# Wider score products, a bank for each PSUM tile, fewer direct down chunks and one final copy, in a cached-attention decode kernel

## The chip, the cores and the metric

The kernel runs on one core of one Trainium2 chip. The metric is the device time of one execution in microseconds. Before the change three runs took 1343.89, 1348.59 and 1349.69 us, with a median of 1348.59 us. The execution whose profile is read here took 1346.37 us, of which 1344.6 us lie between its first and its last instruction (the span).

## The reference

Two sequences, one new token each, go through attention over a cached key and value store, then a gated feed-forward net, and then through both once more with the same weights and caches. Everything is float32.

```python
B, Sq, D = 2, 1, 448;  H, Sk, Dh = 16, 4096, 256;  F = 1792
def A(x, k_cache, v_cache, wq, wo):            # k_cache, v_cache: [B, H, Sk, Dh]
    q = (x @ wq).reshape(B, Sq, H, Dh).transpose(0, 2, 1, 3)
    p = softmax(einsum("bhqd,bhkd->bhqk", q, k_cache) * Dh ** -0.5)
    o = einsum("bhqk,bhkd->bhqd", p, v_cache)
    return o.transpose(0, 2, 1, 3).reshape(B, Sq, H * Dh) @ wo
def F_(x, W_gate, W_up, W_down):
    gate, up = x @ W_gate, x @ W_up
    return (relu(gate) * up) @ W_down
x = x + A(layernorm(x), ...);  x = x + F_(layernorm(x), ...)
x = x + A(layernorm(x), ...);  x = x + F_(layernorm(x), ...)
```

The two caches hold 268 MB together, and each pass over the layers reads nearly all of them.

## The kernel before

**Work units.** One unit of attention is a head of one sequence: 4 MB of keys and 4 MB of values, each in four chunks of 1 MB. A pass has 32 units; the second pass goes through them in the opposite order, so that 22 chunks that the first pass read last can stay in SBUF (`KEPT`). All loads go to one large tile, the `arena`: 27 places of 1 MB, six blocks of four and three single ones.

**Loads.** A list fixes the order of all loads of the program, and SyncE's queue issues them in that order (`pump`, line 127). A load can be issued when its place in the arena has been released, which is when the last product that reads the old contents has run. Most loads of keys and values take a whole block of 4 MB; at the start and the end of a pass they take single chunks. Behind the units of a pass stand the weights of the feed-forward net: seven pieces `w_in`, four pieces `w_out`. At the end of the program nothing has to be released any more for them. In the middle, between the passes, 22 chunks are kept, and the weights go through the few places that are left.

**A unit in the loop** (line 416). `score` (line 303) multiplies the unit's query with a chunk of keys. A chunk holds 1024 keys, cut into two halves j of the head's 256 dimensions and four groups g of 256 keys. Products of one group write one PSUM row, 0, 32, 64 or 96, so that four groups stand in four column groups of the array; the two halves j are summed there. VectorE copies the result to SBUF (`found_s`, line 314), and `score_turn` (line 316) turns it, by a product with a few columns of the identity, so that keys lie on partitions. Then come the maximum and the exponentials, and `weigh` (line 350) multiplies the weights of four times two keys' columns with four pairs of value rows, 512 columns at a time, into `po`. `out_copy` and `out_add` (lines 368, 371) scale the two rows and add them into `row`; in the next unit `out_turn`, `out_keep` and `project` turn that row and multiply it with the output weights into `acc`. TensorE runs its instructions in the order in which they are written: the steps of the unit before (`out_turn`, `out_keep`, `project`) stand behind all four chunks' scores of a unit.

**The feed-forward net** (line 435). `proj` multiplies the normed x with the gate weights into `raw[:, 0]` (lines 447 to 460), then with the up weights into `raw[:, 1]` (line 469); gate and up are multiplied into `row`, transposed into `raw[:, 0]` again and copied back (lines 472 to 485). The down product has 14 chunks of rows. In the first pass all 14 go to `pd` in `raw[:, 1]` (line 517), four column groups side by side, each with 32 columns of weights. In the second pass seven go there; after them ScalarE copies `pd` (line 524), a product (line 250, called from line 525) adds it into the output rows `y`, and the other seven go straight into `y` with two columns each (line 522), all in the same column group. Those seven need an operand that is already scaled (`near`, `near_tails`, lines 496 to 505). At the end VectorE copies half of `y`, ScalarE the other half, and the result is stored (lines 539 to 542).

**Tiles and waits.** `po_all` and `raw` are one tile of two banks each. An instruction that writes one half of such a tile waits until readers of its other half are done.

## Time and profile before

| what | value |
|---|---|
| median of three runs | 1348.59 us (1343.89 to 1349.69) |
| profiled execution, its time and its span | 1346.37 us, 1344.6 us |
| TensorE, VectorE, ScalarE busy | 80%, 15%, 7% of the span |
| data moved by DMA | 562.71 MB, mean 419 GB/s |
| mean granted TensorE clock | 0.74 of full speed |
| score products (line 308) | 4096 instructions, 481 ns each as modelled |
| value products (line 358) | 2048 instructions, 812 ns each as modelled |

A product in float32 stands in the profile as two matmul instructions, each with its weight load. Instructions in four column groups overlap, so that the modelled time of one is several times the distance from one to the next. In a table of windows the columns are: the window, its length, the busy time of each engine with the count of its instructions, the granted TensorE clock, the mean busy share of the 16 DMA engines, and the rate in GB/s. In a timeline a row has its start, its length, the engine, the line and the operands, the count where equal ones are merged, and in brackets the idle time before it with what ended it.

### The profile page before, as it was taken

What the parts mean: (1) busy time and instruction counts of PE and PEld (TensorE: products, weight loads), DVE (VectorE), ACT (ScalarE), POOL (GpSimd) and SP (SyncE); (2) the same over time, 40 slices, a digit from 0 to 9 for tenths busy, and PEclk for the clock granted to TensorE, in tenths of its full rate; (3) what the DMA queues carried; (4) which work ended last, traced back from release to release, by engine and by line L of the source; (5) the groups of instructions that cost most, each with busy time, mean ns of one, the idle gap of its engine ahead of it and who ended that gap; (6) DMA issues with size and microseconds to landing.
All of it is one profiled execution on the core that took longest, in us unless ns stands there. A gap on an engine that the chain in (4) does not pass through costs nothing.

```text
span 1344.6 us, 18672 instructions
## 1 busy us (share of the span) xinstructions
PE 1077.4 (80%) x8328; PEld 476.1 (35%) x8328; DVE 203.3 (15%) x676; ACT 93.4 (7%) x284; POOL 47.7 (4%) x134
## 2 busy tenths in 40 slices
PE   4887889787787787887878988678786788767977
PEld 2434234332332333343334433234242333333432
DVE  1111111111111111111112211111111111111111
ACT  1000000000000000000010000000000000000001
POOL 0000000000000000000000000000000000000000
PEclk9867776667767776766778896876776777677678
DMA  9999999999999999999969999999999999999996
GB/s 398 432 431 431 428 428 432 431 427 428 430 433 432 429 429 427 431 432 421 403 255 400 436 428 431 431 427 431 429 429 434 428 429 429 429 434 429 426 418 252
DMA packets 29607, 562.71 MB, mean 419 GB/s; under 512 B 3284, under 2 KB 3416, under 8 KB 10200
## 3 DMA queue, kind: packets, MB, share of 16 engines
q1 hardware_dynamic: 29524, 561.53, 98.0%
q8 instruction: 65, 1.06, 0.3%
q14 instruction: 14, 0.11, 0.0%
q10 hardware_dynamic: 4, 0.00, 0.0%
HBM read 561.52 MB, written 0.00 MB: 418 GB/s over the span
## 4 chain that ended last, share of the span: by engine, by line
PE 65%; DMA 15%; another core or an unknown queue 14%; DVE 3%; issue 2%; ACT 1%; SPq 0%; POOL 0%; POOLq 0%; DVEq 0%; ACTq 0%
PE raw L308 22%; PE po L358 20%; PE small L321 11%; DMA arena<-in_k_cache_dram 11%; PE pq L283 4%; DMA arena<-in_w_head_dram 4%; PE small L380 2%; PE acc L399 2%; DVE found_s L314 2%; PE pq L286 1%; PE raw L447 1%; DMA arena<-in_w_in_dram 1%; PE raw L517 0%; PE acc L522 0%
## 5 line engine op out<-in xcount | busy, mean ns | idle before, releaser
L308 PE MATMUL raw<-arena,q 128*1 128x256 f32 x4096 | 360.2, 481 | 176.3 <-DMA arena<-in_k_cache_dram 140.0
L358 PE MATMUL po<-arena,probs 128*2 128x512 f32 x2048 | 343.9, 812 | 48.0 <-DMA arena<-in_v_cache_dram 43.1
L308 PEld LDWEIGHTS raw<-arena,q 128*1 128x1 f32 x4096 | 91.9, 91 | 376.3 <-issue 147.1
L321 PEld LDWEIGHTS small<-ident,found_s 128*128 128x128 f32 x1024 | 176.2, 248 | 123.1 <-issue 118.8
L321 PE MATMUL small<-ident,found_s 128*128 128x4 f32 x1024 | 196.2, 301 | 0.3
L314 DVE COPY found_s<-raw 128x256 f32<-128x256 f32 x256 | 108.6, 424 | 475.1 <-PE raw L308 474.6
L358 PEld LDWEIGHTS po<-arena,probs 128*2 128x2 f32 x2048 | 63.7, 103 | 293.3 <-issue 271.8
L372 DVE SCALAR_TENSOR_TENSOR row<-po,ri,row 128x256 f32<-128x256 f32 x64 | 31.0, 484 | 379.8 <-ACT row L369 379.8
L283 PE MATMUL pq<-xs,arena 128*128 128x2 f32 x384 | 71.6, 303 | 0.4 <-DVE xs L246 0.4
L283 PEld LDWEIGHTS pq<-xs,arena 128*128 128x128 f32 x384 | 68.9, 263 | 1.9 <-DVE total L256 1.5
L335 ACT ACTIVATE nm<-top,nsr 128x1 f32<-128x1 f32 x64 | 18.8, 294 | 726.2 <-POOL top L330 726.2
L330 POOL PARTITION_ALL_REDUCE top<-mx x64 | 22.5, 351 | 1184.7 <-DVE mx L328 1152.3
L369 ACT ACTIVATE row<-po,ri 128x256 f32<-128x256 f32 x64 | 30.3, 473 | 446.1 <-PE po L358 446.1
L399 PE MATMUL acc<-arena,oT 128*2 128x448 f32 x128 | 45.5, 804 | 8.1 <-DVE oT L389 8.1
L380 PE MATMUL small<-ones,row 128*128 128x1 f32 x256 | 48.5, 294 | 2.2 <-DVE row L372 2.2
L380 PEld LDWEIGHTS small<-ones,row 128*128 128x128 f32 x256 | 45.8, 252 | 4.9 <-DVE row L372 4.9
L286 PE MATMUL pq<-xs,arena 128*128 128x2 f32 x128 | 30.4, 307 | 0.0
L286 PEld LDWEIGHTS pq<-xs,arena 128*128 128x128 f32 x128 | 28.0, 270 | 0.0
L342 POOL PARTITION_ALL_REDUCE total<-rs x64 | 24.5, 383 | 63.5 <-ACT probs L338 63.5
L338 ACT ACTIVATE probs<-small,nm,sr 128x32 f32<-128x32 f32 x64 | 24.1, 377 | 2.1
L328 DVE TENSOR_REDUCE mx<-small 128x1 f32<-128x32 f32 x64 | 12.3, 191 | 62.9 <-PE small L321 62.9
L447 PE MATMUL raw<-arena,xs 128*32 128x448 f32 x128 | 16.6, 661 | 5.4 <-DMA arena<-in_w_in_dram 3.1
(90 smaller groups left out, 134.9 us busy)
## 6 DMA issues: line engine op xcount, KB each, us to landing
arena<-in_k_cache_dram SPq DMA_DIRECT2D x57, 4096.0 KB, 54.0
arena<-in_v_cache_dram SPq DMA_DIRECT2D x56, 4096.0 KB, 54.0
arena<-in_w_head_dram SPq DMA_DIRECT2D x31, 896.0 KB, 48.8
arena<-in_v_cache_dram SPq DMA_DIRECT2D x22, 1024.0 KB, 19.8
arena<-in_k_cache_dram SPq DMA_DIRECT2D x16, 1024.0 KB, 19.8
arena<-in_w_in_dram SPq DMA_DIRECT2D x14, 896.0 KB, 18.9
arena<-in_w_out_dram SPq DMA_DIRECT2D x4, 896.0 KB, 12.0
arena<-in_w_out_dram SPq DMA_DIRECT2D x3, 672.0 KB, 7.8
```

The lines of the kernel that those rows point to most:

```text
L283: nc.tensor.matmul(pq[:, j, :], w[:, at : at + P], xT[:, c, :], start=(c == 0), stop=False)
L286: nc.tensor.matmul(pq[:, j, :], w[:, FULL * DH : FULL * DH + P], xT[:, FULL + j, :], start=False, stop=True,)
L308: nc.tensor.matmul(raw[32 * g : 32 * g + 1, half, at : at + QN], q_of[u][:, j, :], kt[:, j, g, :], start=(j == 0), stop=(j == 1),)
L314: nc.vector.tensor_copy(found_s[:, half, :], raw[:, half, at : at + QN])
L321: nc.tensor.matmul(s_of[u][:, n : n + G], found_s[:, c % 2, e * P : (e + 1) * P], pick, start=True, stop=True,)
L342: nc.gpsimd.partition_all_reduce(r_of[u], rs, P, RED.add)
L358: nc.tensor.matmul(po_of[u][32 * t : 32 * t + 2, :], p_of[u][:, n : n + 2], vt[:, 2 * t * DH : (2 * t + 2) * DH], start=(c == 0), stop=(c ...
L369: nc.scalar.activation(row[:, :DH], po_of[u][:, :DH], AF.Copy, scale=r_of[u][:, 0:1])
L372: nc.vector.scalar_tensor_tensor(row[:, :DH], po_of.pop(u)[:, DH:], r_of[u][:, 1:2], row[:, :DH], op0=ALU.mult, op1=ALU.add,)
L380: nc.tensor.matmul(pT_of[u][:, c : c + 1], row[:, c * P : (c + 1) * P], ones, start=True, stop=True,)
L399: nc.tensor.matmul(acc[at : at + B], oT_of[h][:, c, :], wo[:, c * D : (c + 1) * D], start=(n < 3), stop=(n >= n_u - 3),)
L447: nc.tensor.matmul(p[32 * j : 32 * j + 32, :], xs[:, c, :], w[:, j * D : (j + 1) * D], start=(n == 0), stop=(n == 3),)
```

## The change

A chunk of keys now holds one half j of the 256 dimensions for four groups of 512 keys, instead of both halves for four groups of 256. So `score` issues four products of 512 columns for a chunk instead of eight of 256, and a sum is complete after two chunks. The host lays the keys out accordingly; the loads keep their sizes and their order. VectorE copies 512 columns twice in a unit instead of 256 columns four times: the first half to `found_s`, the second to `row`. `out_turn`, `out_keep` and `project` of the unit before move up in the order of a unit. `po_all` and `raw` become two tiles each, one for each bank. In the last feed-forward net 11 of the 14 down chunks go to `pd` and three straight to `y`, and the final copy is one ScalarE instruction.

```diff
-G, E = 4, 2
-QN = E * P
+G, E = 4, 4
...
-    po_all = ps_o.tile([P, 2, 2 * DH], F32, name="po")
-    nc.vector.memset(po_all, 0.0)
-
-    raw = ps_r.tile([P, 2, 2 * DH], F32, name="raw")
-    nc.vector.memset(raw, 0.0)
+    po_all = [ps_o.tile([P, 2 * DH], F32, name=f"po{k}") for k in "ab"]
+    raw = [ps_r.tile([P, 2 * DH], F32, name=f"raw{k}") for k in "ab"]
+    for bank in (*po_all, *raw):
+        nc.vector.memset(bank, 0.0)
...
         def score(u, c):
-            kt = get("k", order[u], c).rearrange("p (j g n) -> p j g n", j=2, g=G)
-            half, at = c % 2, c // 2 * QN
-            for j in range(2):
-                for g in range(G):
-                    nc.tensor.matmul(
-                        raw[32 * g : 32 * g + 1, half, at : at + QN],
-                        q_of[u][:, j, :], kt[:, j, g, :], start=(j == 0), stop=(j == 1),
-                    )
+            kt = get("k", order[u], c).rearrange("p (g n) -> p g n", g=G)
+            half, j = c // 2, c % 2
+            for g in range(G):
+                nc.tensor.matmul(
+                    raw[half][32 * g : 32 * g + 1, :], q_of[u][:, j, :], kt[:, g, :],
+                    start=(j == 0), stop=(j == 1),
+                )
             if ("k", order[u], c) not in after:
                 release("k", order[u], c)
-            nc.vector.tensor_copy(found_s[:, half, :], raw[:, half, at : at + QN])
+
+        def score_copy(u, half):
+            nc.vector.tensor_copy(row if half else found_s, raw[half])
...
         for u in range(n_u + 1):
             if_pair(score, u, 0)
-            for c in range(1, NC):
-                if_pair(score, u, c)
-                if_pair(score_turn, u, c - 1)
-            if_pair(score_turn, u, NC - 1)
+            if_pair(score, u, 1)
+            if_pair(score_copy, u, 0)
+            if_pair(out_turn, u - 1)
+            if_pair(out_keep, u - 1)
+            if_pair(score, u, 2)
+            if_pair(score, u, 3)
+            if_pair(score_copy, u, 1)
+            if_pair(score_turn, u, 0)
+            if_pair(project, u - 1)
+            if_pair(score_turn, u, 1)
             if_pair(softmax_max, u)
             if_pair(softmax_exp, u)
-            if_pair(out_turn, u - 1)
-            if_pair(out_keep, u - 1)
-            if_pair(project, u - 1)
...
-            near = row[:, D : D + 12 * B].rearrange("p (m j b) -> p m j b", m=FULL, j=4)
+            near = row[:, D : D + 3 * B].rearrange("p (k b) -> p k b", k=3)
+            last_full = hT[:, 2, 96:].rearrange("p (b r) -> p b r", b=B)[..., 0]
+            nc.vector.tensor_mul(near[:, 0], last_full, square)
...
-        n_pd = 7 if last else 14
+        n_pd = 11 if last else 14
...
-    nc.vector.tensor_copy(found[:, : D // 2], y[:, : D // 2])
-    nc.scalar.activation(found[:, D // 2 :], y[:, D // 2 :], AF.Copy)
+    nc.scalar.activation(found, y, AF.Copy)
```

Three places of TensorE's order follow. The first is an inner unit of the first pass that also has the output weights' product of the unit before (line 399), between the value products of two units (line 358). Before:

```order
L358 MATMUL po<-arena,probs 2x512 x16
L308 MATMUL raw<-arena,q 1x256 x16
L321 MATMUL small<-ident,found_s 128x4 x2
L308 MATMUL raw<-arena,q 1x256 x8
L321 MATMUL small<-ident,found_s 128x4 x2
L308 MATMUL raw<-arena,q 1x256 x8
L321 MATMUL small<-ident,found_s 128x4 x4
L380 MATMUL small<-ones,row 128x1 x2
L399 MATMUL acc<-arena,oT 2x448 x2
L358 MATMUL po<-arena,probs 2x512 x16
```

The same unit now; the new line 305 is `score`, 321 `score_turn`, 380 `out_turn`:

```order
L358 MATMUL pob<-arena,probs 2x512 x16
L305 MATMUL rawa<-arena,q 1x512 x8
L380 MATMUL small<-ones,row 128x1 x2
L305 MATMUL rawb<-arena,q 1x512 x8
L321 MATMUL small<-ident,found_s 128x4 x4
L399 MATMUL acc<-arena,oT 2x448 x2
L321 MATMUL small<-ident,row 128x4 x4
L358 MATMUL poa<-arena,probs 2x512 x16
```

There are 16 products with the keys instead of 32. The turning of the unit before stands between the two halves of the scores instead of behind them, and the turning of the scores stands behind all of them.

The second place is the end of the program on TensorE, from the gate products of the last feed-forward net on. Before:

```order
L447 MATMUL raw<-arena,xs 32x448 x16
L250 MATMUL acc<-row,lead 2x448
L261 MATMUL small<-total,ones 128x2
L447 MATMUL raw<-arena,xs 32x448 x16
L474 MATMUL raw<-ident,row 128x128 x3
L476 MATMUL raw<-ident,row 64x128 x2
L517 MATMUL raw<-arena,row 32x448 x7
L250 MATMUL acc<-row,scaled 2x448
L522 MATMUL acc<-arena,row 2x448 x7
```

Now:

```order
L450 MATMUL rawa<-arena,xs 32x448 x16
L248 MATMUL acc<-row,lead 2x448
L259 MATMUL small<-total,ones 128x2
L450 MATMUL rawb<-arena,xs 32x448 x16
L477 MATMUL rawa<-ident,row 128x128 x3
L479 MATMUL rawa<-ident,row 64x128 x2
L515 MATMUL rawb<-arena,row 32x448 x11
L248 MATMUL acc<-row,scaled 2x448
L520 MATMUL acc<-arena,row 2x448 x3
```

Four products went from the direct kind (line 522, now 520) to the kind of four column groups (line 517, now 515). Gate and up products, and the transposes and the down products, now write different tiles.

The third place is what these instructions wait for, in the same stretch: the first up product, and the first down product. Before:

```order
L447 MATMUL raw<-arena,xs 32x448 [waits Activation_49]
L517 MATMUL raw<-arena,row 32x448 [waits DMAHW1_49,DVE_49,Activation_49]
```

Now the first up product waits for nothing, and the first down product no longer waits for ScalarE:

```order
L450 MATMUL rawb<-arena,xs 32x448 x4
L515 MATMUL rawb<-arena,row 32x448 [waits DMAHW1_49,DVE_49]
```

The queue of SyncE issues the same loads in the same order and with the same waits as before.

32 lines of the change are left out of this document (13 added, 19 removed).

## The prediction

> **What bounds the kernel now.** I read the page first: the slices, the DMA queues, the chain of waits and the costliest groups.
>
> ```profile
> span 1344.6 us, 18672 instructions
> ...
> PE 1077.4 (80%) x8328; PEld 476.1 (35%) x8328; DVE 203.3 (15%) x676; ACT 93.4 (7%) x284; POOL 47.7 (4%) x134
> ...
> DMA  9999999999999999999969999999999999999996
> GB/s 398 432 431 431 428 428 432 431 427 428 430 433 432 429 429 427 431 432 421 403 255 400 436 428 431 431 427 431 429 429 434 428 429 429 429 434 429 426 418 252
> ...
> q1 hardware_dynamic: 29524, 561.53, 98.0%
> q8 instruction: 65, 1.06, 0.3%
> ...
> PE 65%; DMA 15%; another core or an unknown queue 14%; DVE 3%; issue 2%; ACT 1%; SPq 0%; POOL 0%; POOLq 0%; DVEq 0%; ACTq 0%
> ...
> L308 PE MATMUL raw<-arena,q 128*1 128x256 f32 x4096 | 360.2, 481 | 176.3 <-DMA arena<-in_k_cache_dram 140.0
> L358 PE MATMUL po<-arena,probs 128*2 128x512 f32 x2048 | 343.9, 812 | 48.0 <-DMA arena<-in_v_cache_dram 43.1
> ```
>
> The chain gives TensorE 65%, but the slices say otherwise: DMA is full in all of them but the first, the one at the half and the last. The chain steps along TensorE wherever it happens to be busy; it doesn't ask whether that work had to be done by then. The second view, a table of windows, decides between the two:
>
> ```profile
> 34.00:640.00 606.00, 493.75 (x3740) 219.12 (x3736) 87.85 (x283) 37.08 (x120) 22.05 (x60) 0.71 1.00 430
> ...
> 664.00:668.00 4.00, 4.00 (x24) 0.70 (x20) 0.00 (x0) 0.00 (x0) 0.00 (x0) 0.50 1.02 422
> 668.00:680.00 12.00, 9.54 (x61) 4.10 (x54) 2.21 (x11) 2.39 (x4) 0.00 (x0) 0.70 0.51 195
> ...
> 694.00:708.00 14.00, 12.33 (x85) 6.93 (x77) 3.08 (x15) 2.38 (x5) 0.00 (x0) 0.70 0.48 167
> 708.00:1300.00 592.00, 476.45 (x3901) 210.13 (x3904) 90.88 (x293) 38.30 (x124) 22.75 (x62) 0.75 1.00 429
> ```
>
> For 606 and again for 592 us the DMA engines' share is 1.00, at 430 GB/s, whatever TensorE does. So the time is two streams of loads, a hole between them in which the feed-forward net runs, and the work behind the last values. TensorE's busy time inside the streams costs nothing. I look for what the change does to the streams, to the hole and to the end.
>
> **Part 1: scores, copies, order of a unit: nothing, by cover.** Score instructions fall from 4096 to 2048, with the width of the value products: at that row's 343.9 us for 2048, TensorE saves about 16 us of busy time, and some waits for copies between chunks. The cover is the stream itself. VectorE's copies go from four to two a unit; at 15% busy it has room. `out_turn` now stands before the third chunk's scores, and it waits for `out_copy` and `out_add`, half a microsecond each; two chunks of scores run meanwhile. Without that cover some 0.5 us a unit would go into TensorE's slack, not into the time. Loads are issued by the same releases in the same order.
>
> **Part 2: instruction fetch.** This is the one thing in the streams that I expect to move. The page has 16,656 matmuls and weight loads; at 1.06 MB the queue that fetches instructions brings 64 bytes for each, in 65 packets of 16 KB. Now 2048 products fewer in both kinds leave 12,560, or 49 packets. What does a packet cost the stream? By its own time, 0.3% of 16 engines over 1344.6 us, 65 engine-microseconds, 1 us each. The end of the program shows more:
>
> ```profile
> 1326.00:1334.00 8.00, 5.26 (x52) 1.92 (x54) 2.10 (x8) 1.13 (x4) 0.00 (x0) 1.00 0.66 272
> ...
> 1332.00:1334.00 2.00, 0.97 (x11) 0.40 (x14) 0.92 (x4) 0.43 (x2) 0.00 (x0) 1.00 0.50 201
> 1334.00:1336.00 2.00, 1.35 (x8) 0.17 (x3) 0.00 (x0) 0.54 (x1) 0.00 (x0) 1.00 0.02 7
> ```
>
> All loads had been issued by then, yet the share falls to 0.50: half of the engines are done, the others late. The idle part is 0.34 x 8 us x 16 = 43.5 engine-microseconds; if eight engines are late, they are late by 5.4 us. A load counts as landed when its last engine is done, so the late ones set the stream. The fetches of a pass, asked of the first stream (the second one answers the same), are
>
> ```profile
> q8 instruction: 31, 0.51, 0.3%
> ```
>
> 31 packets on eight engines are four on each, so 1.4 us a packet would explain the lateness. With 8 packets fewer in a pass the late engines have three each: the last values land 1.4 us earlier in each pass, -2.8 us in all. Bounds: nothing, if the lateness has another source; at most 3.2 us, if the stretch of half rate is read as 6.4 us long. I take 2.8, since the count fits.
>
> **Part 3: the hole.** The chain there:
>
> ```profile
> 675.05 4.21 PE raw L447 x24
> 679.28 8.30 DMA arena<-in_w_in_dram
> ...
> 704.01 1.93 PE raw L308 x9
> ```
>
> The up products now write their own bank and needn't wait for ScalarE's read of the gate; but here they wait for weights that can't be issued before the gate products release their places. So that gain is hidden by the load of 8.30 us. The stream starts again when the first chunk of the second pass has been scored; with 8 instructions for 16 in a stretch of 1.93 us I take -0.3, between 0 and -1.0.
>
> **Part 4: the end.** After the last values nothing hides TensorE's work. The timeline:
>
> ```profile
> 1325.78 0.38 PE L261 MATMUL small<-total,ones 128*128 128x2 f32 x2
> ...
> 1326.94 3.21 PE L447 MATMUL raw<-arena,xs 128*32 128x448 f32 x32 [0.78 <-ACT row L468]
> ...
> 1331.94 0.56 DVE L480 COPY row<-raw 128x384 f32<-128x384 f32 x1 [1.02 <-PE raw L476]
> ...
> 1333.03 1.70 PE L517 MATMUL raw<-arena,row 128*32 128x448 f32 x14 [1.14 <-ACT row L485]
> ...
> 1334.79 0.54 ACT L524 ACTIVATE row<-raw 128x448 f32<-128x448 f32 x1 [1.81 <-PE raw L517]
> ...
> 1336.14 5.42 PE L522 MATMUL acc<-arena,row 128*2 128x448 f32 x14
> ...
> 1341.67 0.40 DVE L540 COPY row<-acc 2x224 f32<-2x224 f32 x1 [8.49 <-PE acc L522]
> 1342.10 0.35 ACT L541 ACTIVATE row<-acc 2x224 f32<-2x224 f32 x1 [6.76 <-DVE row L540]
> 1342.47 0.33 SPq L542 DMA_DIRECT2D out_dram<-row  x1
> ```
>
> - Up products start behind line 261, without ScalarE: -0.78 (the idle time in the row). Their last weights are the rows below: issued at 1309.43, landed about 1328.3 by the median of these loads, needed by the last 8 of 32 instructions at 1326.2 + 2.4 = 1328.6. That just fits.
> - Down products wait for VectorE's copy alone. It ends at 1332.50; with the 0.05 us of such a handover they start at 1332.55 instead of 1333.03: -0.48.
> - Eight more instructions side by side. 14 take 1.70 us, the last one about 0.4 of it; so 0.1 us from one to the next, +0.8. But the third piece of down weights must be there: about +0.1.
> - Eight fewer instructions on one column group: 5.42 us for 14, again with 0.5 for the last, makes 0.375 each: -3.0.
> - One copy: from 1341.56 to 1342.45 it was 0.89 us. ScalarE's copy of 448 columns took 0.54 and starts 0.06 behind TensorE: -0.29.
>
> Issues and landings, first of the last up weights, then of the third piece of down weights (start; KB and the time from issue to landing):
>
> ```profile
> 1309.43 0.33 SPq L127 DMA_DIRECT2D arena<-in_w_in_dram  x1
> arena<-in_w_in_dram SPq DMA_DIRECT2D x7, 896.0 KB, 18.9
> ...
> 1316.28 0.33 SPq L127 DMA_DIRECT2D arena<-in_w_out_dram  x1
> arena<-in_w_out_dram SPq DMA_DIRECT2D x1, 896.0 KB, 16.8
> ```
>
> The third piece lands at 1333.1. The down products now start at 1332.55 - 0.78 = 1331.8 and need it 1.3 us later, at 1333.1: no margin, hence the 0.1. The last pieces are needed at 1335.5; the share of 0.02 behind 1334 says that they are in by then. The sum is -0.78 - 0.48 + 0.9 - 3.0 - 0.29 = -3.65; I take -3.7, between -3.0 (the third piece 0.7 late) and -4.0.
>
> **Sum.** -2.8 - 0.3 - 3.7 = -6.8 us, on the profiled execution 1346.37 - 6.8 = 1339.6. The median of the three runs stands 2.2 us above that execution, so by the median it is 1341.8. I forecast 1341.5, faster by 0.5%. That is just about what a measurement of this kernel can tell from no change.
>
> **Rivals.**
> - *Fetch costs nothing, or is spread over 16 engines.* Lateness may come from elsewhere, say from engines that are slower for all loads. For it: no row names the engine of a packet. Then the sum is -4.0; with 16 packets of 1.4 us spread over 16 engines it is -5.4. That is 1344.6 or 1343.2; I say 1344.
> - *TensorE bounds after all.* For it: 65% of the chain. Then the 16 us of busy time come off beside the 3.7 of the end: 1329 or less. Against it: a share of 1.00 in 1198 of 1344.6 us. [...] The DMA share speaks against it here.
> - *A colder clock at the end.* The stretch from 1326 on ran at a granted clock of 1.00. [...] Compare the same 32 instructions of line 447, for the gate, a few microseconds earlier:
>
> ```profile
> 1320.20 4.90 PE L447 MATMUL raw<-arena,xs 128*32 128x448 f32 x32 [0.36 <-DVE xs L246]
> ```
>
> 4.90 against 3.21: 1.5 times as long. On some 10 us of TensorE's work that is +5 us; the gain shrinks to 1.8 us and the time is 1347. [...]
> - *Slower: the clock falls in the streams, until TensorE can't follow them.* A unit is 8.39 MB, 19.5 us at 430 GB/s. TensorE's 1077.4 us less 16 are 16.6 us a unit at a mean clock of 0.74. Were all of it bound by the clock, it would reach 19.5 at 0.63. At 0.60 a unit takes 20.5, and 64 units lose 1.0 us each; the loads in flight cover part of it once. The time would be near 1390. For it: the clock did fall to 0.50 for stretches. [...]
>
> **Chances.** Forecast 0.60, no gain from fetch 0.20, cold end 0.12, TensorE bound 0.04, slower 0.04. Faster by over 0.5% means below 1341.85, which cuts the forecast's own spread (1339 to 1344) a little above its middle: 0.4 of its 0.60, plus 0.04 and 0.01 of the fetch rival, make 0.45. Slower is 0.04, the rest 0.51. The range is 1336 to 1346.5. Below: the upper bounds of fetch, hole and end (-3.2, -1.0, -4.0) make 1340.4, and the lowest of the three runs stood 4.7 us under their median. Above: fetch at nothing makes 1344.6, the highest run stood 1.1 over the median, and 0.8 goes to a part of the cold end.
>
> **What would show it.** Right: 49 fetch packets and 0.80 MB; a DMA share still at 1.00 in both streams; the last values' wait ending about 2.8 us earlier plus what the hole gives; half rate at the end for about 4 us instead of over 5; first up product directly behind line 259; six instructions of line 520; one copy of 0.54 us. Wrong: last values that land as late as before, which kills part 2; a clock below 1.00 behind 1326; a gap before the third piece of the down weights; a share below 1.00 in a stream. The forecast fails as a whole if the streams' rate differs by more than 0.3% from the one that is read here.

## The result, and the profile after

The changed kernel takes 1339.72 us (median of 6 runs, 1337.56 to 1341.76), against 1347.93 us for the kernel before (6 runs, 1343.89 to 1349.69). The ratio is 0.9941, with a 95% interval of 0.9924 to 0.9959. The forecast was 1341.5 us. The profiled execution took 1339.52 us, with a span of 1337.7 us; the sum had put that execution at 1339.6.

The page after, in the same parts as the page before:

```profile
span 1337.7 us, 14371 instructions
...
PE 1020.2 (76%) x6280; PEld 377.6 (28%) x6280; DVE 182.7 (14%) x549; ACT 93.6 (7%) x284; POOL 47.7 (4%) x134
...
DMA  9999999999999999999979999999999999999997
...
q1 hardware_dynamic: 29524, 561.53, 98.4%
q8 instruction: 49, 0.80, 0.2%
...
PE 71%; another core or an unknown queue 15%; DMA 8%; issue 2%; ACT 2%; DVE 1%; POOL 1%; POOLq 0%; ACTq 0%; DVEq 0%
...
L305 PE MATMUL rawa<-arena,q 128*1 128x512 f32 x1024 | 180.1, 833 | 173.3 <-DMA arena<-in_k_cache_dram 173.2
```

The queue that fetches instructions (q8) carries 49 packets and 0.80 MB, where it had 65 and 1.06. The data are the same to the packet. TensorE is 57.2 us less busy and waits more for keys (173.2 us in the row above, 140.0 before); its part of the chain still grew, from 65% to 71%. That is why the chain was not taken for the bound: TensorE lost 57 us of work and the span shrank by 6.9.

The table of windows after (window, length, busy time of PE, PEld, DVE, ACT, POOL, clock, DMA share, GB/s):

```profile
34.00:640.00 606.00, 467.34 (x2772) 171.87 (x2768) 77.38 (x221) 36.30 (x117) 21.27 (x58) 0.73 1.00 430
668.00:680.00 12.00, 10.17 (x72) 3.77 (x72) 2.66 (x14) 2.61 (x5) 0.00 (x0) 0.86 0.60 219
694.00:708.00 14.00, 12.84 (x70) 7.45 (x69) 3.29 (x15) 2.38 (x5) 0.00 (x0) 0.63 0.54 204
708.00:1300.00 592.00, 451.82 (x2884) 164.22 (x2884) 80.44 (x231) 38.30 (x124) 22.74 (x62) 0.76 1.00 429
...
1324.00:1326.00 2.00, 2.00 (x28) 0.52 (x16) 0.03 (x1) 0.00 (x0) 0.00 (x0) 1.00 0.94 381
1326.00:1328.00 2.00, 1.18 (x11) 0.51 (x7) 0.62 (x1) 0.00 (x0) 0.00 (x0) 1.00 0.63 259
1328.00:1330.00 2.00, 1.34 (x18) 0.58 (x19) 0.96 (x4) 0.44 (x2) 0.00 (x0) 1.00 0.50 205
1330.00:1332.00 2.00, 1.35 (x13) 0.21 (x5) 0.00 (x0) 0.54 (x1) 0.00 (x0) 1.00 0.11 42
```

Both streams still run at a share of 1.00 and 429 to 430 GB/s. At the end the share is near a half from 1326 to 1330, about 4 us.

To see where the 6.9 us went, I cut each span at three events that a trace shows: the landing of a pass's last values, SyncE's first issue of keys for the second pass, and its issue of the output's store. In the timeline of before the last values' wait ends at 1311.89, and the second stream starts here:

```profile
705.96 0.33 SPq L127 DMA_DIRECT2D arena<-in_k_cache_dram  x1
...
1311.89 0.10 PEld L358 LDWEIGHTS po<-arena,probs 128*2 128x2 f32 x4 [0.86 <-DMA arena<-in_v_cache_dram]
1311.91 2.52 SPq L127 DMA_DIRECT2D arena<-in_w_out_dram  x2
```

In the timeline of after the issue that comes directly behind the last values' landing stands 3.63 us earlier:

```profile
703.75 0.33 SPq L126 DMA_DIRECT2D arena<-in_k_cache_dram  x1
...
1308.28 2.52 SPq L126 DMA_DIRECT2D arena<-in_w_out_dram  x2
```

All runs cut in this way are in one table. It is worked out from the records of each profiled execution: the landing is the last completion of the last load of values; "streams" is the time up to the first such landing plus the time from the second pass's first issue to the second landing; the hole lies between; the end runs from the second landing to the issue of the store. Some 2.1 us behind that issue belong to the span. The last two columns are of all runs of the kernel, not of that execution; each ratio is to runs of the kernel before that were made beside them (their medians lie between 1347.93 and 1349.24 us).

| kernel (label) | fetch packets | streams | hole | end | span | median us | ratio to before, interval |
|---|---|---|---|---|---|---|---|
| before | 65 | 1272.60 | 39.25 | 30.62 | 1344.6 | 1347.93 | |
| changed | 49 | 1269.47 | 38.75 | 27.39 | 1337.7 | 1339.72 | 0.9941 (0.9924 to 0.9959) |
| changed, again (e0_changed) | 49 | 1269.49 | 38.88 | 26.75 | 1337.2 | 1339.07 | 0.9925 (0.9909 to 0.994) |
| 256-column scores (e1_halves) | 65 | 1272.62 | 39.49 | 26.75 | 1341.0 | 1341.72 | 0.995 (0.9935 to 0.9965) |
| 128-column scores (e2_quarters) | 97 | 1278.19 | 40.46 | 27.36 | 1348.1 | 1348.2 | 0.9992 (0.9982 to 1.0001) |
| fewer products (e3_fewer) | 29 | 1266.35 | 35.61 | 26.80 | 1330.9 | 1335.05 | 0.9898 (0.9884 to 0.9913) |
| before + end (e4_end) | 65 | 1272.55 | 39.25 | 29.66 | 1343.6 | 1346.89 | 0.9994 (0.9981 to 1.0007) |
| before + banks (e5_banks) | 65 | 1272.52 | 36.49 | 28.12 | 1339.2 | 1343.13 | 0.9956 (0.9943 to 0.9969) |
| before + banks, again (e11_banks_again) | 65 | 1272.58 | 38.60 | 28.11 | 1341.4 | 1344.58 | 0.9966 (0.9953 to 0.998) |
| before + scores (e6_scores) | 49 | 1269.02 | 39.16 | 29.98 | 1340.3 | 1341.28 | 0.9946 (0.9931 to 0.9961) |
| 14 chunks in groups (e8_all14) | 49 | 1269.34 | 37.28 | 26.05 | 1334.8 | 1338.03 | 0.9927 (0.9911 to 0.9944) |
| banks merged (e9_merged) | 49 | 1269.29 | 37.93 | 27.46 | 1336.8 | 1339.68 | 0.9947 (0.9928 to 0.9965) |
| idle products (e10_warm) | 50 | 1269.40 | 36.95 | 26.76 | 1335.2 | 1337.33 | 0.992 (0.9903 to 0.9938) |
| idle products, 14 chunks (e12_warm14) | 50 | 1269.28 | 38.62 | 26.04 | 1336.1 | 1336.6 | 0.9913 (0.9899 to 0.9928) |

From before to the change the streams gave 3.1 us (forecast 2.8), the hole 0.5 (0.3) and the end 3.2 (3.7).

The chain of waits through the hole after:

```profile
672.68 3.88 PE rawa L450 x24
676.58 7.90 DMA arena<-in_w_in_dram
684.52 1.58 PE rawb L450 x8
686.11 6.90 DMA arena<-in_w_out_dram
...
702.01 2.56 PE rawa L305 x12
```

The 8.30 us wait for up weights is still there with 7.90, and where TensorE's own down products of 4.92 us stood before, a second wait for weights has come, of 6.90 us. A faster TensorE in the middle of the hole would meet loads.

The timeline of the end after:

```profile
1306.58 4.46 PE L358 MATMUL pob<-arena,probs 128*2 128x512 f32 x24
...
1317.19 4.88 PE L450 MATMUL rawa<-arena,xs 128*32 128x448 f32 x32 [0.36 <-DVE xs L244]
...
1322.76 0.38 PE L259 MATMUL small<-total,ones 128*128 128x2 f32 x2
...
1323.07 3.21 PE L450 MATMUL rawb<-arena,xs 128*32 128x448 f32 x32
...
1328.68 2.46 PE L515 MATMUL rawb<-arena,row 128*32 128x448 f32 x22 [0.66 <-DVE row L483]
...
1332.54 2.42 PE L520 MATMUL acc<-arena,row 128*2 128x448 f32 x6
...
1335.05 0.54 ACT L538 ACTIVATE row<-acc 2x448 f32<-2x448 f32 x1 [3.32 <-PE acc L520]
1335.61 0.33 SPq L539 DMA_DIRECT2D out_dram<-row  x1
```

Up products come directly behind line 259, the 22 instructions of the down products side by side run without a gap, and the six direct ones take 2.42 us. Only the first rows are less good than before: when the last values land, at 1308.22, TensorE is still at work on earlier ones, and the gate products start 1317.19 - 1308.22 = 8.97 us behind the landing, where before it was 1320.20 - 1311.85 = 8.35.

### The profile page after: what moved, and what is told of

Its sections match the earlier page's. It is cut to its first block, busy times and chain, and to the rows that moved or that the text cites. A ratio compares the mean times of both kernels' runs of the same rounds, so it can differ in the third digit from the quotient of the medians.

```text
span 1337.7 us, 14371 instructions
## 1 busy us (share of the span) xinstructions
PE 1020.2 (76%) x6280; PEld 377.6 (28%) x6280; DVE 182.7 (14%) x549; ACT 93.6 (7%) x284; POOL 47.7 (4%) x134
## 4 chain that ended last, share of the span: by engine, by line
PE 71%; another core or an unknown queue 15%; DMA 8%; issue 2%; ACT 2%; DVE 1%; POOL 1%; POOLq 0%; ACTq 0%; DVEq 0%
PE pob L358 13%; PE rawa L305 12%; PE poa L358 12%; PE rawb L305 11%; PE small L321 10%; DMA arena<-in_k_cache_dram 4%; PE pq L281 4%; DMA arena<-in_v_cache_dram 4%; PE small L380 3%; PE acc L399 2%; PE pq L284 1%; ACT probs L338 1%; POOL top L330 1%; PE rawa L450 1%
## 5 line engine op out<-in xcount | busy, mean ns | idle before, releaser
L305 PE MATMUL rawa<-arena,q 128*1 128x512 f32 x1024 | 180.1, 833 | 173.3 <-DMA arena<-in_k_cache_dram 173.2
L358 PE MATMUL pob<-arena,probs 128*2 128x512 f32 x1024 | 182.5, 877 | 52.1 <-DMA arena<-in_v_cache_dram 48.8
L358 PE MATMUL poa<-arena,probs 128*2 128x512 f32 x1024 | 174.8, 845 | 59.9 <-ACT probs L338 42.6
L305 PE MATMUL rawb<-arena,q 128*1 128x512 f32 x1024 | 166.2, 775 | 0.0
L321 PEld LDWEIGHTS small<-ident,found_s 128*128 128x128 f32 x512 | 71.7, 216 | 76.4 <-issue 76.4
L313 DVE COPY found_s<-rawa 128x512 f32<-128x512 f32 x64 | 44.3, 692 | 285.6 <-PE rawa L305 285.6
L358 PEld LDWEIGHTS pob<-arena,probs 128*2 128x2 f32 x1024 | 30.5, 108 | 173.2 <-issue 168.9
L321 PE MATMUL small<-ident,found_s 128*128 128x4 f32 x512 | 77.3, 274 | 0.0
L321 PEld LDWEIGHTS small<-ident,row 128*128 128x128 f32 x512 | 69.6, 211 | 25.7 <-issue 25.7
L321 PE MATMUL small<-ident,row 128*128 128x4 f32 x512 | 74.1, 268 | 0.0
L313 DVE COPY row<-rawb 128x512 f32<-128x512 f32 x64 | 44.3, 692 | 147.0 <-PE rawb L305 147.0
```

What stands on the lines that cost most here:

```text
L305: nc.tensor.matmul(raw[half][32 * g : 32 * g + 1, :], q_of[u][:, j, :], kt[:, g, :], start=(j == 0), stop=(j == 1),)
L313: nc.vector.tensor_copy(row if half else found_s, raw[half])
L321: nc.tensor.matmul(s_of[u][:, n : n + G], rows[:, e * P : (e + 1) * P], pick, start=True, stop=True,)
L358: nc.tensor.matmul(po_of[u][32 * t : 32 * t + 2, :], p_of[u][:, n : n + 2], vt[:, 2 * t * DH : (2 * t + 2) * DH], start=(c == 0), stop=(c ...
```

## The experiments

The theory: in the streams only the fetched instructions cost time, the end gives the sum of its edits, the hole nearly nothing. The rivals: lateness has another source than fetch; the clock, not the edits, sets hole and end.

### The changed kernel again

No edit. It tells how far one kernel's parts differ from one execution to the next.

> The changed kernel again, as the mark for the runs beside it on the same chip. 0.994 of the time before; 49 fetch packets; the loads of the last values landing about 1.5 us earlier in each pass than before the change, with the late engines about 5 us behind the early ones at the end instead of 6.7.

Measured: 1339.07 us (1335.35 to 1339.75). Streams and hole agree with the first profile within 0.15 us. The end is 0.64 us shorter, though its products had to wait; in its timeline:

```profile
1329.67 0.96 PE L515 MATMUL rawb<-arena,row 128*32 128x448 f32 x8 [0.85 <-DMA arena<-in_w_out_dram]
```

TensorE reached the down products earlier and stood 0.85 us for the third piece of their weights. That load is the floor of this end: 26.75 us here and in e1_halves, 26.76 in e10_warm, and in all three these products wait for it. The margin that the prediction called none is none.

### Instruction fetch: 65, 97 and 29 packets

Three kernels change the number of instructions in the streams and leave loads and end as they are. The first cuts the score products of the changed kernel into halves again, on the old layout of the keys:

```diff
-            kt = get("k", order[u], c).rearrange("p (g n) -> p g n", g=G)
-            half, j = c // 2, c % 2
-            for g in range(G):
-                nc.tensor.matmul(
-                    raw[half][32 * g : 32 * g + 1, :], q_of[u][:, j, :], kt[:, g, :],
-                    start=(j == 0), stop=(j == 1),
-                )
+            kt = get("k", order[u], c).rearrange("p (j g n) -> p j g n", j=2, g=G)
+            half, at = c // 2, c % 2 * DH
+            for j in range(2):
+                for g in range(G):
+                    nc.tensor.matmul(
+                        raw[half][32 * g : 32 * g + 1, at : at + DH],
+                        q_of[u][:, j, :], kt[:, j, g, :], start=(j == 0), stop=(j == 1),
+                    )
...
```

> The changed kernel, with each score product of 512 columns cut into two of 256 (and the keys laid out for it as before the change): the same arithmetic, copies, waits, banks and end, but 4096 instructions more on TensorE, so 65 fetch packets again. If instruction fetch makes eight engines late: one packet more on each in either pass, each stream 1.4 to 1.6 us longer, +3 us on the time of the changed kernel (ratio to the kernel before about 0.997), and the half-rate stretch at the end over 6 us again. If fetch costs nothing and the streams became shorter through the wider products or the order: 0 us. If TensorE bounds: +16 us or more, the busy time that comes back.

The second cuts them into quarters of 128 columns:

```diff
...
+            for s in (0, P):
+                for j in range(2):
+                    for g in range(G):
+                        nc.tensor.matmul(
+                            raw[half][32 * g : 32 * g + 1, at + s : at + s + P],
+                            q_of[u][:, j, :], kt[:, j, g, s : s + P],
+                            start=(j == 0), stop=(j == 1),
+                        )
...
```

> The same with four products of 128 columns for each of 512: 97 fetch packets, so 48 more than the changed kernel, three more on each late engine in either pass. If fetch makes the engines late, step by step: each stream 4.2 to 4.8 us longer, +9 us against the changed kernel, ratio to the kernel before about 1.001, and the engines at the end 9 to 10 us apart. If fetch costs nothing: 0 us, as long as the DMA share stays at 1.00. If TensorE, now with many more short instructions, can't follow the loads, the DMA share in the streams falls below 1.00 and the time grows by tens of us.

The third has fewer products than the change: it leaves out three of the four groups of scores and half of the value products, so that what it computes is not the attention.

```diff
-            for g in range(G):
+            for g in range(1):
...
-            for t in range(CT // 2):
+            for t in range(CT // 4):
```

> The changed kernel with three of the four groups of score products and half of the value products left out (so what it computes is not the attention): 5120 instructions fewer on TensorE, about 29 fetch packets instead of 49, while every load stays. If fetch makes the engines late: two packets on each late engine in a pass instead of three, each stream 1.4 to 1.6 us shorter, -3 us against the changed kernel. If fetch costs nothing: 0 us. If TensorE bounds: far more, since the products of a third of its busy time are gone: over 100 us.

Measured: with 65 packets the streams take 1272.62 us, as before the change (1272.60); with 97 they take 1278.19, with 29 1266.35. The fetch queue of the kernel with quarters, from its page (packets, MB, share of 16 engines):

```profile
q8 instruction: 97, 1.59, 0.5%
```

Its windows, the first stream and then the end:

```profile
34.00:640.00 606.00, 434.92 (x5540) 242.79 (x5536) 76.56 (x219) 36.29 (x117) 21.27 (x58) 0.77 1.00 429
...
1332.00:1334.00 2.00, 2.00 (x20) 0.68 (x16) 0.14 (x1) 0.43 (x2) 0.00 (x0) 1.00 0.62 250
1334.00:1336.00 2.00, 2.00 (x28) 0.65 (x20) 0.35 (x3) 0.26 (x1) 0.00 (x0) 1.00 0.50 207
...
1338.00:1340.00 2.00, 1.34 (x17) 0.60 (x20) 0.95 (x4) 0.44 (x2) 0.00 (x0) 1.00 0.48 199
1340.00:1342.00 2.00, 1.52 (x18) 0.28 (x8) 0.00 (x0) 0.42 (x1) 0.00 (x0) 1.00 0.24 91
```

TensorE's products are busy for 434.92 us of the first 606, less than in the changed kernel (467.34), and the share of the DMA engines is 1.00 in both; yet its streams are 8.7 us longer. In the kernel with 29 packets TensorE has 1604 matmul instructions in the same window instead of 2772 and is as busy by the profile, 466.46 us; so it is a test of the packets, and the 100 us that were expected of it if TensorE bounds can't be tested by it. What follows the packets is the stretch at half rate: some 8 us here, 4 after the change, over 5 before. So the late engines are late by the instructions that they fetch, and TensorE's time in the streams is free.

The price: from 65 to 97 packets 5.6 us, 0.17 each; from 49 to 65 3.1 us, 0.20 each; from 29 to 49 3.1 us, 0.16 each. In the medians the three kernels lie 2.7, 9.1 and -4.0 us from the changed kernel beside them (1339.07), where +3, +9 and -3 were expected. The last one's hole is shorter too, 35.61 us; its first scores have fewer instructions, and how much of that is clock isn't shown. Counted as the prediction did, with the packets of a pass (14, 23, 31, 47) dealt to eight engines, the busiest one gets 2, 3, 4 and 6; then one more on it costs 1.6, 1.6 and 1.4 us a pass. Both counts fit. That there are eight engines is read from the share of 0.50 and from the durations of the packets, which repeat with a period of eight in the records (1.07, 1.06, 1.10, 1.10, 1.09, 1.03, 1.02, 1.08 us in the changed kernel); no record names a packet's engine.

The completions tell more. Each load has 16 of them in the records. For the last load of values of the first pass, the first eight come at 661.1 to 661.5 us on average, whether the pass fetched 14, 23, 31 or 47 packets; the other eight come at 663.0, 664.5, 666.3 and 669.1 us. So half of a load's completions are late, and only that half moves with the packets. With 23, 31 and 47 packets seven of the late ones stand together, and the eighth is 1.1 to 1.5 us ahead of them: each of these numbers is one short of a multiple of eight. That is what packets dealt in turn to eight engines would give.

A packet is 16 KB: 0.80 MB in 49 of them. For the loads beside them 16 packets more, from 49 to 65, are 3.1 us more. Whether TensorE ever stands for its own code these runs don't show.

### The scores alone

The kernel before with the wide score products and the new order of a unit, but two-bank tiles and the old end:

```diff
-G, E = 4, 2
-QN = E * P
+G, E = 4, 4
...
+                nc.tensor.matmul(
+                    raw[32 * g : 32 * g + 1, half, :], q_of[u][:, j, :], kt[:, g, :],
+                    start=(j == 0), stop=(j == 1),
+                )
```

> The kernel before with the wide score products and the new order of a unit alone, two banks in one tile and the old end: the complement of the other two. If fetch is what moves the streams: 49 packets, -3.2 us in the two streams, about -0.4 in the hole, 0 to +0.6 at the end (in the changed kernel the last value products ended 0.6 us later behind their landing than before), so -3 to -3.6, ratio 0.9975. If the banks were needed for the streams' gain: 0.

Measured: 1341.28 us. The streams take 1269.02 us, 3.6 less than before; hole 39.16 and end 29.98 are within 0.7 us of before. So this part alone carries the gain of the streams; the other two parts do nothing there (1272.55 and 1272.52). In the span that is 4.3 us. By the medians it is more, 7.2 us (1348.52 for the kernel before beside it), a ratio of 0.9946 where 0.9975 was expected; where the rest comes from is not shown.

### The end alone, and all 14 chunks in four groups

The kernel before with the edits of the last feed-forward net alone:

```diff
-        n_pd = 7 if last else 14
+        n_pd = 11 if last else 14
...
-    nc.vector.tensor_copy(found[:, : D // 2], y[:, : D // 2])
-    nc.scalar.activation(found[:, D // 2 :], y[:, D // 2 :], AF.Copy)
+    nc.scalar.activation(found, y, AF.Copy)
```

> The kernel before with the edits of its end alone: 11 down chunks side by side and three straight to the output rows, and one final copy. By the sum: eight instructions moved, -3.0 and +0.8, the copy -0.29, so -2.5 us at the end (from the last values' landing to the last store), ratio 0.998; both streams as before the change, 65 fetch packets, last values landing as before. If the third piece of the down weights came too late there would be a gap in front of its products; without the banks' gain they start 1.3 us later than in the changed kernel, so I expect none.

Measured: 1346.89 us, not to be told from before (1348.52 beside it). Nine of its ten runs took 1345.35 to 1348.67 us; the tenth, with a mean clock of 0.638 where the nine had 0.737 to 0.749, took 1353.18. The end is 29.66 us instead of 30.62. The sum had it at 28.1. A window of this kernel shows why it isn't:

```profile
1333.70:1337.10 3.40, 3.30 (x18) 0.61 (x10) 0.00 (x0) 0.06 (x1) 0.00 (x0) 0.50 0.03 12
```

and the down products in its timeline:

```profile
1332.95 4.05 PE L512 MATMUL raw<-arena,row 128*32 128x448 f32 x22 [1.14 <-ACT row L485]
```

The same 22 instructions that take 2.46 us after the change took 4.05 here, as the granted clock fell to 0.50 for 3.4 us in the middle of them. At the duration of 2.46 the end would be 28.07 us: the edits are worth 2.55 us, and one stretch of half clock took 1.59 of it.

The other one goes further than the change: all 14 down chunks in the four column groups, none direct.

```diff
-        n_pd = 11 if last else 14
+        n_pd = 14
...
-                else:
-                    nc.tensor.matmul(y, near[:, k - n_pd], w_k, start=False, stop=(k == 13))
                 if last and k == n_pd - 1:
                     nc.scalar.activation(row[:, :D], pd, AF.Copy)
-                    add_rows(P, scaled)
+                    add_rows(P, scaled, stop=True)
```

> The changed kernel with all 14 down chunks side by side in the last feed-forward net, none straight to the output rows: six direct instructions fewer at 0.375 us, six more side by side at 0.1 us: -2.25 + 0.6 = -1.65 us at the end, if the last two pieces of the weights are there. In the changed kernel they landed at 1330.6 and 1331.1 and would now be needed at about 1330.9 and 1331.3: just in time. If they come late, the gain shrinks by what they are late. Against the kernel before: 0.993.

Measured: 1338.03 us, and an end of 26.05 us, 0.70 below the floor of the changed kernel. The timeline:

```profile
1327.87 0.96 PE L504 MATMUL rawb<-arena,row 128*32 128x448 f32 x8 [0.57 <-DMA arena<-in_w_out_dram]
1329.03 1.44 PE L504 MATMUL rawb<-arena,row 128*32 128x448 f32 x6 [0.20 <-DMA arena<-in_w_out_dram]
```

Two waits for the last two pieces of weights, 0.57 and 0.20 us, stand in it. From the first profile of the changed kernel the end is 1.34 us shorter, where 1.65 were expected. In time the two can't be told apart (0.9927 against 0.9925 and 0.9941).

### The banks: alone, alone again, and undone

The kernel before with one tile for each bank, run twice:

```diff
-    po_all = ps_o.tile([P, 2, 2 * DH], F32, name="po")
-    nc.vector.memset(po_all, 0.0)
-
-    raw = ps_r.tile([P, 2, 2 * DH], F32, name="raw")
-    nc.vector.memset(raw, 0.0)
+    po_all = [ps_o.tile([P, 2 * DH], F32, name=f"po{k}") for k in "ab"]
+    raw = [ps_r.tile([P, 2 * DH], F32, name=f"raw{k}") for k in "ab"]
+    for bank in (*po_all, *raw):
+        nc.vector.memset(bank, 0.0)
...
```

> The kernel before with one tile for each bank alone. By the sum: the up products start 0.78 us earlier at the end, the down products another 0.48: -1.26 us behind the last values, ratio 0.999; nothing in the hole, where the up products wait for weights; nothing in the streams, though the waits of the score products for copies go away. If these waits bounded, the time would fall by the 35 us that TensorE spends in them.

> The kernel before with the bank split alone, once more, to see whether its profiled hole repeats. Theory A, a program's pattern of clock windows repeats from one execution to the next: hole 36.5 us and end 28.1 us again (before: 39.25 and 30.62), time 4 to 6 us under the kernel before. Theory B, the pattern of that one execution was chance: the hole lies anywhere between 36.5 and 40 us, and the time comes to 1.3 to 4 us under the kernel before.

The changed kernel with the opposite edit, two-bank tiles again:

```diff
-    po_all = [ps_o.tile([P, 2 * DH], F32, name=f"po{k}") for k in "ab"]
-    raw = [ps_r.tile([P, 2 * DH], F32, name=f"raw{k}") for k in "ab"]
+    po_all = ps_o.tile([P, 2, 2 * DH], F32, name="po")
+    raw = ps_r.tile([P, 2, 2 * DH], F32, name="raw")
...
```

> The changed kernel with its four one-bank tiles put back together as two tiles of two banks, as they stood before; scores, order and end as changed. Theory A, the sum of the prediction: the program keeps 49 fetch packets, both streams and the hole stay as in the changed kernel (hole 38.8 us from the last values of pass 1 to the first key load of pass 2), and the up and down products at the end wait for ScalarE again, +1.26 us there (27.4 to about 28.6), so about +1.3 us in all. Theory B, the banks are worth what they gave when put alone into the kernel before (-5.4 us in the profiled span, of it -2.8 in the hole and -2.5 at the end): about +5 us, of it +2.8 in the hole.

Measured: the first profile of the banks alone gave 5.4 us, 2.8 of it in the hole. The second gave 3.2: its hole is 38.60 us instead of 36.49, with the same program. The same window of the two, the first one's row and then, in the second fence, the other's:

```profile
671.80:678.60 6.80, 6.33 (x45) 2.60 (x46) 1.57 (x9) 1.34 (x2) 0.00 (x0) 0.75 0.54 206
```

```profile
671.80:678.60 6.80, 5.71 (x34) 3.07 (x36) 1.57 (x9) 1.91 (x3) 0.00 (x0) 0.51 0.27 101
```

A clock of 0.75 in one execution and 0.51 in the other, and TensorE 11 matmul instructions further on. So the 2.1 us between the two holes came from the clock of that execution, not from the program.

At the end both gave 2.5 us, twice the 1.26 of the sum. The gate products of the second one start 1317.51 - 1311.18 = 6.33 us behind the last values, 2.0 sooner than before, where the clock had stood at half until 1.5 us past the landing:

```profile
1299.80:1313.40 13.60, 12.82 (x76) 5.25 (x72) 1.59 (x6) 0.76 (x3) 0.73 (x2) 0.50 1.01 419
```

In the second run of the banks it was back at 1.00 at 1310.3, 0.9 us ahead of the landing. Without ScalarE's wait its last up products then waited for weights, 0.86 us.

In the time the banks alone gave more than their rows: 5.4 us in the nine runs of the first kernel, 3.9 in the ten of the second (1348.52 and 1348.43 for the kernel before beside them). The rows of the banks explain 1.26 of it; the rest is not shown.

In the kernel with merged banks the two waits are back, in the size that the sum had given them:

```profile
1314.03 5.78 PE L451 MATMUL raw<-arena,xs 128*32 128x448 f32 x32 [0.36 <-DVE xs L245]
...
1321.66 3.21 PE L451 MATMUL raw<-arena,xs 128*32 128x448 f32 x32 [0.79 <-ACT row L472]
...
1327.75 2.46 PE L516 MATMUL raw<-arena,row 128*32 128x448 f32 x22 [1.14 <-ACT row L489]
```

0.79 and 1.14 - 0.66 = 0.48 make 1.27 us. Yet its end is 27.46 us, against 27.39 with separate banks, and its time is 1339.68 us. Its gate products started 1314.03 - 1307.22 = 6.81 us behind the last values, 2.16 sooner than in the changed kernel's first profile, and took 0.90 longer: -2.16 + 0.90 + 1.27 = 0.01. So in the changed kernel the banks' gain is real in the rows and can't be seen in the time: neither the +1.3 us of the sum nor the +5 of the banks alone came. From this execution's end down to the floor of 26.75 there was 0.7 us to gain.

### Products of no use in the waits

If the clock in hole and end follows TensorE's activity, keeping TensorE busy should raise it. The changed kernel with 44 products that nobody reads, in places where TensorE waits:

```diff
+    def warm(n, width=2 * DH):
+        for _ in range(n):
+            for g in range(4):
+                nc.tensor.matmul(
+                    po_all[0][32 * g : 32 * g + 32, :width], ident[:, :32], found_s[:, :width],
+                    start=True, stop=True,
+                )
...
+        warm(1, DH)
         absorb(acc[:SUMS], SUMS, lead, nlead)
...
+                if not last and half and n == 1:
+                    warm(4)
...
```

> The changed kernel with 44 more products of no use (eleven groups of four side by side, 256 or 512 columns, into a bank of PSUM that nobody reads at that time), placed where TensorE waits in the hole and at the end. Theory A, the granted clock in these stretches follows how busy TensorE has been in the few microseconds before: the clock of 0.63 to 0.88 in the hole rises towards 1.00, the hole shrinks from 38.8 us to 36.5 or less, and the work behind the last values keeps to its loads at 26.8 us; -2 to -3 us in all. Theory B, the clock changes in windows that don't follow so short a filling: the hole stays within 0.5 us of 38.8, and the fillers themselves cost up to 1 us; 0 to +1 us in all.

Measured: 1337.33 us. The hole fell to 36.95 us, the clock in it stood at 1.00 for the first 28.4 of them, and the end came to the floor of the weights, 26.76. That looked like the first theory, though the hole missed its 36.5 and the time, 1.7 us under that of e0_changed, its 2 to 3. The last kernel has the same products and all 14 chunks in groups, and is the same program up to the last down products:

> The changed kernel with the products of no use and with all fourteen down chunks side by side, both together. Expected if the two add: both streams as in the changed kernel, the hole again near 37 us (36.95 with the products of no use alone), and the end at the landing of the last piece of down weights, 26.05 us as with the fourteen chunks alone, against 26.76: a profiled span near 1334.5 us and a time near 1336.7 us, 0.8 to 0.9% under the kernel before. If the clock in the hole had been luck in that one execution: a hole of 38 to 39 us and a time near 1338.5 us.

Measured: 1336.6 us (1336.13 to 1337.84, 5 runs), with the end at 26.04 us and the time as expected, but with a hole of 38.62; the profiled execution was the slowest of the five. Three windows of e10_warm:

```profile
664.50:667.90 3.40, 2.08 (x20) 0.89 (x20) 0.53 (x2) 0.47 (x1) 0.00 (x0) 1.00 1.01 412
667.90:671.30 3.40, 2.62 (x24) 1.57 (x24) 1.08 (x7) 1.91 (x3) 0.00 (x0) 1.00 0.70 293
671.30:674.70 3.40, 3.36 (x33) 1.04 (x34) 0.60 (x4) 0.00 (x0) 0.00 (x0) 1.00 0.59 196
```

and its gate products in the timeline:

```profile
671.34 3.40 PE L461 MATMUL rawa<-arena,xs 128*32 128x448 f32 x32 [0.36 <-DVE xs L252]
```

The same three windows of e12_warm14:

```profile
664.50:667.90 3.40, 2.65 (x28) 0.89 (x20) 0.51 (x2) 0.48 (x1) 0.00 (x0) 1.00 1.03 420
667.90:671.30 3.40, 2.62 (x24) 1.57 (x24) 1.08 (x7) 1.92 (x3) 0.00 (x0) 1.00 0.72 299
671.30:674.70 3.40, 3.33 (x20) 0.99 (x24) 0.63 (x5) 0.00 (x0) 0.00 (x0) 0.50 0.46 135
```

and its gate products:

```profile
671.37 4.85 PE L461 MATMUL rawa<-arena,xs 128*32 128x448 f32 x32 [0.36 <-DVE xs L252]
```

The same 32 instructions started 0.03 us apart and took 3.40 and 4.85 us, because one window of 3.4 us was granted 1.00 in one execution and 0.50 in the other. TensorE was as busy in the window before (2.62 us in both), and in the one before that it was busier in the execution that then fell to 0.50. This one window explains 1.45 of the 1.67 us between the two holes. So the clock does move the length of the hole, and the products of no use don't settle the clock. The medians of the two kernels with them are the lowest of the unshortened ones, but their intervals overlap those of the changed kernel: whether they help is open.

## Why the prediction came out as it did

**Part 1, nothing by cover: right, though TensorE's own gain was mis-sized.** The share stayed at 1.00, and what TensorE saved came out of its slack. It was 57.2 us where the prediction read 16. The scores gave about that (360.2 us before, 180.1 + 166.2 = 346.3 after); the turning of the scores on line 321, which the prediction left out, gave 44.8 (196.2 before, 77.3 + 74.1 after). That the new order costs nothing in the streams is shown by the scores alone: 3.6 us less, the whole gain of the streams.

**Part 2, fetch: right in mechanism, a little small.** Forecast -2.8, measured -3.1 in the profile, and with the scores halved again all of it came back (+3.1). The price of 1.4 us for one more packet on a late engine measured 1.4 to 1.6. The rival in which fetch costs nothing falls with it. The rival of packets spread over 16 engines falls by its number (1.4 us where 3.1 were measured) and by the completions, of which only half move. By the times alone one smooth price for a packet, 0.16 to 0.20 us, can't be told from the rounds on eight engines; the one completion that comes 1.1 to 1.5 us ahead of the late seven speaks for the rounds.

**Part 3, the hole: the value near, the bounds wrong.** -0.3 forecast, -0.5 measured. But the step that set its range at 0 to -1.0 held TensorE's speed there to be given; the same program gave 36.49 and 38.60 us. In the hole the clock moves more than all edits together, so that -0.5 came near -0.3 is luck.

**Part 4, the end: every edit as priced, 0.5 us lost ahead of them.** By the rows: -0.78 for the up products, -0.48 for the down products (0.66 for 1.14), 2.46 - 1.70 = +0.76 for eight more side by side, 2.42 - 5.42 = -3.00 for the direct ones; for the copy, from the end of the last product at 1334.96 to the end of ScalarE's row at 1335.59, 0.63 for 0.89, -0.26. That is -3.76. The gate products started 0.62 us later behind the last values, which leaves -3.1; the other 0.1 is spread over rows that differ by a few hundredths. The term that was missing is this one: the prediction let nothing change between the last values and the gate products, but TensorE was still on earlier values when the last ones landed. The 24 instructions it then ran took 4.46 us, at a clock of 0.51 from 1307.0 to 1310.4; in e12_warm14 the same 24 took 2.76. Over the fourteen executions of the table the gate products start 6.33 to 9.15 us behind the last values; before (8.35) and the change (8.97) are both among the late ones, and the kernel with the scores alone stands at 6.60. So this distance is no steady cost of the change, and the 3.2 us of the end hold for these two executions. The third piece of weights was in time in this execution and 0.85 us late in the next, so the 0.1 set aside for it was too little.

**The rivals.** TensorE as the bound: shown wrong by the quarters, where it is less busy and the streams longer. The cold clock at the end: in the kernel before, the 32 gate products of 4.90 us were granted 0.50 for their first 3.4 us, to 1323.6, and 1.00 for the rest. It came again, but as one or two windows of 3.4 us, worth 0.6 us against before in the changed kernel and 1.6 in the kernel with the end alone, not the 5 us of the estimate; what brought it is not shown. The clock falling in the streams until TensorE can't follow: it stood at 0.73 and 0.76, and nothing came of it. Only the one run of the kernel with the end alone, at 0.638, was 6.7 us above the median of its others; it has no trace.

**The median.** The sum was made on one execution. Before, the median of six lies 1.6 us above that execution; after, 0.2. So the medians differ by 8.2 us where the spans differ by 6.9. In the repeat beside e0_changed the medians differ by 10.2. What made the profiled execution of before one of the quicker ones isn't shown; the clock in the hole, which moved it by 2.1 us between two executions of one program, would be enough. Nor do the medians of the parts add up as the rows do: the scores alone gave 7.2 us, the banks 3.9 and 5.4, the end 1.6, more together than the whole change. The rows account for the profiled executions, and 1 to 3 us of the gain in the medians stay unexplained. That the sum met the profiled execution to 0.1 us (1339.6 and 1339.52) is luck as well: streams and hole gave 0.5 us more than forecast and the end 0.5 less.

## What to carry to other kernels

Where the DMA engines are full, count the packets of the instruction queue: each is a load too, and an instruction that is saved saves time there even on an engine with slack (here 16 packets fewer were 3.1 us, with TensorE's products busy for 467 to 494 of 606 us). Where they are not full, price each edit by its rows, and then ask which load lands next; here a floor of 26.75 us behind the last values took what was left. And before a gain of one or two microseconds in a short stretch is put down to an edit, run the same program twice and compare the granted clock in that stretch.

## What the hardware did that I had not expected

In the clock records of all fourteen executions the granted clock stands only at 0.50 or 1.00, and each stretch lasts a multiple of 3.41 us, but for one in each that the profile cuts off. A stretch in which TensorE is busy throughout, as the profile counts busy time, can still stand at the lower of the two; in the changed kernel, in the second stream:

```profile
1280.00:1290.00 10.00, 10.00 (x46) 4.30 (x38) 1.54 (x3) 0.00 (x0) 0.00 (x0) 0.50 1.02 424
```

Busy for 10.00 of 10 us, at half the clock throughout. What the clock follows, these runs don't show. What it is worth they do: a window at 0.50 cost 1.45 us at the gate products and 1.59 at the down products.

The second surprise is how much the code itself weighs. 16 packets of 16 KB, 0.26 MB of 562, were 3.1 us in a program that moves 0.26 MB in 0.6 us at its 430 GB/s. The price is five times the bytes. The completions of the last values say why: half of them come late by the packets, and the wait for the load ends with the last one (1311.85 before, where TensorE went on at 1311.89).
